# Head memsets, a scaling moved off GpSimd, and the last block's chain in the list scheduler: one change to a fused attention and MLP kernel

## The chip, the cores and the metric

The kernel runs on one core of a Trainium2 chip. A core has TensorE (PE, matrix products into PSUM), VectorE (DVE), ScalarE (ACT), GpSimd (POOL), SyncE (SP, which here only issues transfers) and 16 DMA engines. The metric is the device time of one execution in microseconds. A profile of one execution comes with it; its times count from the start of the profiled span.

## The reference

The input x has 2048 rows of 512 numbers in bf16. It is normalised, goes through an attention of 32 heads of width 16 and, beside it, through a mixer that normalises once more and multiplies along the rows. All three are added.

```python
xn = _layernorm(x)
# attention: H = 32, Dh = 16, no mask
qkv = (xn @ wqkv).reshape(B, S, 3, H, Dh).transpose(2, 0, 3, 1, 4)
p = softmax(einsum("bhqd,bhkd->bhqk", q, k) * Dh ** -0.5)
a = einsum("bhqk,bhkd->bhqd", p, v) -> (B, S, 512) @ wo
# mixer along the rows: F = 1376
u = gelu(einsum("bsd,sf->bdf", _layernorm(xn), w1) + b1)
y = (einsum("bdf,fs->bds", u, w2) + b2).transpose(0, 2, 1)
return x + a + y
```

## The kernel before

**Tiling.** The attention is cut into 32 blocks: 4 query blocks of 512 rows by 8 groups of 4 heads. A block goes over 16 key tiles of 128 rows; each gives two score tiles of 128 keys by 2 heads by 512 queries, so there are 32 x 16 x 2 = 1024 score tiles of 128x1024, numbered n. For each one TensorE writes scores into one of three PSUM slots (L741). ScalarE takes the exponential into a bf16 buffer (L765), or VectorE makes an approximate one: an integer conversion with a bias (L776) and then three copies of it shifted by constants, on VectorE (L785) or GpSimd (L782, an `int64_add` from a library that GpSimd must load first). All four terms are multiplied with V and summed, the last with VM, a scaled copy of V. So a score tile costs one group of P V products (four of 128x256, L808) if ScalarE took it and four groups if VectorE did. V and VM hold 17 columns a head: 16 of values and a one, which makes the softmax sum come out as a 17th row. Where two of the four heads' columns have to be zero, V and VM are cleared.

**Order.** Nothing is scheduled on the chip. A class `Sched` keeps one list of instructions per engine, works out the semaphores from which tile each reads and writes, and keeps a planned time for every engine from written costs. VectorE and GpSimd operations marked `port` are planned not to overlap; beyond the plan, a GpSimd operation waits for the last marked VectorE operation that was emitted ahead of it. Three stretches are written:

1. The head. x tiles are loaded by SP and ScalarE's queue; the first four are normalised (`ln_stats`, `ln_rstd` on GpSimd with a power, `ln_norm` at L549 on VectorE), transposed by TensorE and projected. GpSimd writes ones into V (L659) and zeros into VM (L458, L460); VectorE writes zeros into V (L446, L448).
2. Block 0, in 16 fixed periods, one per key tile: two score tiles, two exponentials on ScalarE, two groups of P V products, and `block0_work`, which normalises, transposes and projects the key tiles two to five ahead. After periods 2, 8, 12 and 15 `vm_scale` (L618) fills VM from V on GpSimd. After period 13 `ln2_stats` (L557 to L561) prepares the second normalisation on GpSimd, whose factors 16 VectorE operations (L565) apply later. After the last period, `late_consts` loads GpSimd's library, clears wo_t on GpSimd (L499), and has SP load wo_c and, into the cleared wo_t, parts of wo; two loads of w1 follow.
3. The list-scheduled loop, for blocks 1 to 31 and the mixer. At each step it collects what each engine could do next, estimates starts, and emits the earliest. Besides scores, exponentials and P V products it handles tasks that are Python generators: Q, K and V projections, the mixer's products, and `task_epilogue`, one per block. The epilogue copies the block's result out of PSUM (L1012), has SP move the softmax sums into dcomp (`den_in`, four transfers) and the values into oC (`o_in`, eight), takes the reciprocal (L1027), writes it to DRAM (`den_mid`), reads it back spread out into denb (`den_out`, four), and after each second block multiplies (two operations at L1048). For block 30, the second-last, it multiplies on its own, half of the rows.

Where the plan leaves TensorE idle and no mixer or projection task is open, it issues products whose result nobody reads (fillers, L1333 and L1339).

Whether VectorE may take a score tile is tested with `n % BN > D_LAST`, with BN = 32 and D_LAST = 31.

After the loop come the standard library on GpSimd and `tail`, which finishes block 31 by itself: VectorE transposes the result (L1075), takes the reciprocal of its sums (L1078), and for each of two halves spreads them out by a transpose (L1082) and multiplies (L1085). TensorE multiplies with wo_t and wo_c into four PSUM banks (L1101, L1090), VectorE (L1113) and ScalarE (L1110) add the rest, and four transfers write the last 512 rows.

The softmax here doesn't subtract the row's maximum and nothing guards it: scores larger than these inputs give would overflow.

## Time and profile before

| | us |
|---|---|
| Median of 3 runs (lowest, highest) | 697.96 (697.03, 698.59) |
| The profiled execution's own time | 698.68 |
| Its span, first to last instruction | 696.9 |
| PE busy in the span | 678.8 (97%) |
| ACT busy | 673.2 (97%) |
| DVE busy | 621.3 (89%) |
| POOL busy | 402.2 (58%) |

A row of the profile's costliest groups gives a line, an engine, an operation, what it writes and reads with the shapes, and a count; then the busy time of all of them in us, the mean of one in ns, the time in which the engine stood idle just before them, and what ended most of that. In a row of the timeline, the first number is the start and the second the duration; what stands in brackets is idle time ahead of it. A row of the chain that ended last gives a start, a duration and what filled it. PE counts as busy when its pipelined products overlap, so its 97% is not a measure of its peak. GpSimd's durations are rough.

### The profile page before, as it was taken

Reading aid. Unit: us, or ns where it says so; the run is one execution under the profiler, and the core shown is the slowest. Engines: PE = TensorE matmul, PEld = TensorE weight load, DVE = VectorE, ACT = ScalarE, POOL = GpSimd, SP = SyncE. Lnnn points to the kernel's source line nnn. Section 1 sums busy time; section 2 is a strip of 40 time slices with the busy share of each in tenths; the row PEclk is TensorE's granted clock in tenths of the full one; section 3 lists DMA queues with packets and bytes.
Section 4 is the critical chain, followed back from the end, with each engine's and each line's share of the span. In section 5 each row is a group of like instructions: output and inputs, shape, how many; then the busy total and the mean of one; then the engine's idle time right before and its main releaser. Section 6 shows DMA issues by size and latency. Waiting matters only on the chain.

```text
span 696.9 us, 29358 instructions
## 1 busy us (share of the span) xinstructions
PE 678.8 (97%) x12916; PEld 312.0 (45%) x12916; DVE 621.3 (89%) x894; ACT 673.2 (97%) x736; POOL 402.2 (58%) x683
## 2 busy tenths in 40 slices
PE   7999999999999999999999999999999999999997
PEld 4433545445544444444444444444444444444443
DVE  7968998998989999989999999898998888888987
ACT  4999999999999999999999999999999999999993
POOL 4544556665356755756666576665766665654642
PEclk9999999999999999999999999999999999999999
DMA  7104200031102200022220212222220222213101
GB/s 211 33 4 82 54 22 20 19 72 28 25 13 52 47 23 19 19 55 46 50 39 22 48 38 54 53 56 53 52 60 20 54 54 57 70 35 81 45 23 44
DMA packets 85728, 32.32 MB, mean 46 GB/s; under 512 B 67424, under 2 KB 85600, under 8 KB 85600
## 3 DMA queue, kind: packets, MB, share of 16 engines
q1 hardware_dynamic: 85168, 30.05, 18.6%
q8 instruction: 101, 1.65, 1.0%
q10 hardware_dynamic: 432, 0.39, 0.2%
q14 instruction: 27, 0.22, 0.1%
HBM read 21.76 MB, written 2.35 MB: 35 GB/s over the span
## 4 chain that ended last, share of the span: by engine, by line
PE 80%; ACT 12%; DVE 4%; DMA 2%; issue 1%; POOL 0%; SPq 0%; DVEq 0%
PE ps L808 32%; PE ps L741 29%; PE ps L839 15%; ACT pT L765 8%; ACT x_sb L765 3%; PE ps L893 2%; DMA denb<-rden_scratch 1%; DVE pT L776 1%; DVE OT L1012 1%; ACT gT_sb L950 1%; DVE hx L549 0%; SPq L431 0%; DMA x_sb<-in_A_x_dram 0%; PE ps L590 0%; DVE oT L1048 0%
## 5 line engine op out<-in xcount | busy, mean ns | idle before, releaser
L765 ACT ACTIVATE pT<-ps 128x1024 bf16<-128x1024 f32 x535 | 523.2, 1132 | 3.3 <-PE ps L741 2.7
L776 DVE TENSOR_SCALAR pT<-ps 128x1024 int16<-128x1024 f32 x221 | 270.1, 1222 | 26.8 <-PE ps L741 20.8
L741 PE MATMUL ps<-QT,KT 32*128 32x512 bf16 x2048 | 284.8, 385 | 5.3 <-ACT pT L765 3.5
L782 POOL INT64_ADD pT<-pT x299 | 181.6, 616 | 129.5 <-DVE pT L785 74.2
L808 PE MATMUL ps<-pT,V 128*32 128x256 bf16 x4716 | 243.8, 276 | 2.9 <-DVE OT L1012 2.5
L765 ACT ACTIVATE x_sb<-ps 128x1024 bf16<-128x1024 f32 x182 | 197.9, 1141 | 0.2 <-PE ps L741 0.2
L741 PEld LDWEIGHTS ps<-QT,KT 32*128 32x128 bf16 x2048 | 78.8, 91 | 183.5 <-ACT pT L765 76.3
L808 PEld LDWEIGHTS ps<-pT,V 128*32 128x32 bf16 x4716 | 107.9, 96 | 85.8 <-issue 66.8
L782 POOL INT64_ADD x_sb<-pT x146 | 89.3, 616 | 57.0 <-DVE pT L785 32.7
L776 DVE TENSOR_SCALAR x_sb<-ps 128x1024 int16<-128x1024 f32 x86 | 105.1, 1222 | 14.7 <-PE ps L741 11.8
L808 PE MATMUL ps<-x_sb,V 128*32 128x256 bf16 x1836 | 116.7, 275 | 1.0 <-DVE OT L1012 0.6
L782 POOL INT64_ADD pT<-x_sb x132 | 79.9, 614 | 48.2 <-DVE pT L785 32.6
L785 DVE TENSOR_SCALAR pT<-pT 128x1024 int16<-128x1024 int16 x154 | 65.1, 426 | 4.5
L808 PE MATMUL ps<-pT,VM 128*32 128x256 bf16 x880 | 61.3, 275 | 0.5 <-DVE pT L785 0.5
L839 PE MATMUL ps<-gT_sb,wblk 128*32 128x512 bf16 (+1 forms) x704 | 61.2, 383 | 0.0
L808 PEld LDWEIGHTS ps<-x_sb,V 128*32 128x32 bf16 x1836 | 46.2, 96 | 31.0 <-issue 23.5
L839 PE MATMUL ps<-hx,wblk 128*32 128x512 bf16 x594 | 52.4, 383 | 0.0
L782 POOL INT64_ADD x_sb<-x_sb x47 | 28.6, 614 | 23.8 <-DVE pT L785 8.0
L847 PE MATMUL ps<-hx,wblk 32*128 32x512 bf16 (+1 forms) x96 | 37.1, 387 | 0.0
L785 DVE TENSOR_SCALAR x_sb<-pT 128x1024 int16<-128x1024 int16 x64 | 27.1, 428 | 1.8
L808 PEld LDWEIGHTS ps<-pT,VM 128*32 128x32 bf16 x880 | 23.3, 96 | 10.6 <-issue 8.8
L785 DVE TENSOR_SCALAR pT<-x_sb 128x1024 int16<-128x1024 int16 x58 | 24.5, 423 | 1.6
(113 smaller groups left out, 460.4 us busy)
## 6 DMA issues: line engine op xcount, KB each, us to landing
wblk<-in_B_w_dram SPq DMA_DIRECT2D x10, 512.0 KB, 4.4
wblk<-in_B_w_dram SPq DMA_DIRECT2D x16, 320.0 KB, 3.6
oC<-OT SPq DMA_DIRECT2D x248, 16.0 KB, 1.8
denb<-rden_scratch SPq DMA_DIRECT2D x124, 32.0 KB, 2.3
xr<-in_A_x_dram SPq DMA_DIRECT2D x16, 128.0 KB, 2.6
dcomp<-OT SPq DMA_DIRECT2D x124, 2.0 KB, 1.7
QT<-Qall SPq DMA_DIRECT2D x120, 16.0 KB, 1.8
out_dram<-osb SPq DMA_DIRECT2D x14, 128.0 KB, 2.0
```

Source lines behind the costliest of these rows:

```text
L741: specs.append(dict(eng="pe", fn=lambda e, r=r, bk=bk: e.matmul(bank(bk), lhsT=KT[32 * r:32 * r + 32, T, 128 * kt:128 * (kt + 1)], rhs=QT[ ...
L765: return [dict(eng="act", fn=lambda e: e.activation(buf(pbuf[n]), ps[:, s_ * 1024:(s_ + 1) * 1024], ACTF.Exp, scale=LN2_128), reads=[("ban ...
L776: return dict(eng="dve", fn=lambda e: e.tensor_scalar(buf_i(w), ps[:, s_ * 1024:(s_ + 1) * 1024], IBIAS, 0.0, ALU.add, ALU.max), reads=[(" ...
L782: return dict(eng=eng, fn=lambda e: e.int64_add(buf_i(o).bitcast(I64), buf_i(w).bitcast(I64), SHIFTS[k] * 0x0001000100010001), reads=[("pT ...
L785: return dict(eng=eng, fn=lambda e: e.tensor_scalar(buf_i(o), buf_i(w), float(SHIFTS[k]), 1.0, ALU.add, ALU.mult), reads=[("pT", w)], writ ...
L808: specs.append(dict(eng="pe", fn=lambda e, c=c, h=h, i=i, off=off: e.matmul(bank(PV_BANK)[32 * c:32 * c + 32, 256 * par:256 * par + 256], ...
L839: specs.append(dict(eng="pe", fn=lambda e, c=c, w=w: e.matmul(bank(EX_BANK)[32 * c:32 * c + w, :], lhsT=lhs_of(32 * c, 32 * c + w), rhs=rh ...
L847: return [dict(eng="pe", fn=lambda e: e.matmul(bank(EX_BANK)[0:dst_rows, :], lhsT=lhs_of(0, dst_rows)[rs], rhs=rhs[rs], start=begin, stop= ...
L893: return [dict(eng="pe", fn=lambda e, ct=ct, c=c: e.matmul(bank(EX_BANK)[32 * c:32 * c + 32, 128 * i:128 * (i + 1)], lhsT=xnT[:, ct, 128 * ...
L950: yield "act", [dict(eng="act", fn=lambda e, ap=ap: e.activation(ap, ap, ACTF.Gelu_apprx_tanh), reads=[("gT", f) for f in fts], writes=[(" ...
L1012: yield "pvev", [dict(eng="dve", fn=lambda e: e.tensor_copy(OT32[:, eb, :], bank(PV_BANK)), reads=[("bank", PV_BANK)], writes=[("OT32", eb)])]
```

## The change

The diff has these parts.

- The ones of V (L659) and the zeros of wo_t (L499) are written by VectorE at the very start. The zeros of V are written by GpSimd, in a function that also does VM's: V's before the first statistics, VM's at the old place.
- The first normalisation is emitted before the statistics of tile 3, the other three after them.
- `vm_scale` of periods 12 and 15 goes to VectorE. `ln2_stats` and `late_consts` are both called after period 12.
- A score tile is kept from VectorE if `n >= 1022`, in place of the old test.
- The epilogue's `o_in` transfers become a generator of their own. For block 30 it runs beside the rest of the epilogue; for the others it runs inside it as before. A new gate makes the multiplication wait, in the plan, for the emission of these transfers.
- The chain of block 31 on VectorE moves from `tail` into `task_last`, which the loop schedules like other tasks.
- The planner keeps a list of the last eight busy intervals of the shared port for each engine instead of one time until which it is taken.
- PER_LIST is 16, the number of periods, so the tests against it leave the periods as they are, and `next_n` starts at 32 as before.

```diff
-D_LAST = 31
+D_END = 1022
@@ Sched
-    def port_time(self, eng, t):
-        return max(t, self.port_free["pool" if eng == "dve" else "dve"])
+    def port_time(self, eng, t, dur):
+        for a, z in self.port_iv["pool" if eng == "dve" else "dve"]:
+            if t < z and t + dur > a:
+                t = z
+        return t
...
-            self.port_free[eng] = op.t0 + cost[0]
+            self.port_iv[eng] = self.port_iv[eng][-7:] + [(op.t0, op.t0 + cost[0])]
@@ head
-        for T in range(1, 4):
-            sc.add("dve", lambda e, T=T: e.memset(v17_kh[:, :, 8 * T, 0:16], 0.0),
-                   writes=[("V", t, T) for t in range(NT)], cost=(0.15, 0.2))
-        sc.add("dve", lambda e: e.memset(V17[:, NKT * H * 17:], 0.0), writes=[("V", NKT, 0)], cost=(0.06, 0.1))
+        sc.add("dve", lambda e: e.memset(v17_main[:, :, 16:17], 1.0), writes=[("Vone",)], cost=(0.5, 0.55))
+        sc.add("dve", lambda e: e.memset(wo_t[:], 0.0), writes=[("wo_t", z) for z in range(4)], cost=(0.92, 0.97))
...
-        def late_memsets():
+        def zero_memsets(nm, whole, kh):
             for T in range(1, 4):
-                sc.add("pool", lambda e, T=T: e.memset(vm_kh[:, :, 8 * T, 0:16], 0.0),
-                       writes=[("VM", t, T) for t in range(NT)], cost=(0.3, 0.4))
-            sc.add("pool", lambda e: e.memset(VM[:, NKT * H * 17:], 0.0), writes=[("VM", NKT, 0)], cost=(0.1, 0.2))
+                sc.add("pool", lambda e, T=T: e.memset(kh[:, :, 8 * T, 0:16], 0.0),
+                       writes=[(nm, t, T) for t in range(NT)], cost=(0.3, 0.4))
+            sc.add("pool", lambda e: e.memset(whole[:, NKT * H * 17:], 0.0), writes=[(nm, NKT, 0)], cost=(0.1, 0.2))
...
             load_lib(INT64_LIB)
-            sc.add("pool", lambda e: e.memset(wo_t[:], 0.0), writes=[("wo_t", z) for z in range(4)], cost=(1.75, 1.8))
...
+        zero_memsets("V", V17, v17_kh)
         ln_sums(1)
...
         ln_rstd(1, 2)
+        ln_norm(0)
         ln_stats(3)
-        sc.add("pool", lambda e: e.memset(v17_main[:, :, 16:17], 1.0), writes=[("Vone",)], cost=(2.28, 2.33))
-        for t in range(NPRE):
+        for t in range(1, NPRE):
             ln_norm(t)
-        late_memsets()
+        zero_memsets("VM", VM, vm_kh)
@@ block 0
-                vm_scale(list(range(4 * j, 4 * j + 4)), 0)
-            if period == 13:
+                vm_scale(list(range(4 * j, 4 * j + 4)), 0, "pool" if period < LN2_AT else "dve")
+            if period == LN2_AT:
                 ln2_stats()
-        late_consts()
+                late_consts()
@@ task_epilogue
-            yield "gate", lambda: p < 2 or PAIRS[p - 2] in oT_done
-            for c in range(4):
-                h, i = divmod(c, 2)
-                for a in range(2):
-                    ro = 64 * e_ + 32 * a + 16 * i
-                    yield "sp", [dict(dst=oC32[ro:ro + 16, tb_, 256 * h:256 * h + 256],
-                                      src=OT32[32 * c:32 * c + 16, eb, 256 * a:256 * a + 256],
-                                      reads=[("OT32", eb)], writes=[("oC32", tb_, e_, c, a)], name="o_in")]
-            yield "call", lambda: ot_free.add(b)
+            g_in = dict(gen=task_o_in(b), cur=None)
+            if b == NBLK - 2:
+                yield "call", lambda: (step_gen(g_in), frees.append(g_in))
+            else:
+                yield from task_o_in(b)
...
+            yield "gate", lambda: b in ot_free and (half or b - 1 in ot_free)
@@ the loop
-                    if n % BN > D_LAST or (qi == 0 and len(ready_q) == 1 and False):
+                    if n >= D_END:
                         continue
...
                     if pv_block == NBLK - 1:
                         pv_block += 1
+                        g = dict(gen=task_last(), cur=None)
+                        step_gen(g)
+                        frees.append(g)
```

`task_o_in` holds the gate and the eight transfers as they stood; `task_last` holds the six VectorE operations of `tail` (transpose, reciprocal, and twice the spreading transpose and the product) as they stood, each as a task step. LN2_AT is 12.

## The prediction

> **What bounds the kernel now.** I read the page's engine rows first, then its costliest groups, then the chain that ended last at both ends of the run, then the timeline where the chain shows a hole. All clock times below are microseconds from the span's start in the profile of before.
>
> ```profile
> PE 678.8 (97%) x12916; PEld 312.0 (45%) x12916; DVE 621.3 (89%) x894; ACT 673.2 (97%) x736; POOL 402.2 (58%) x683
> ...
> L765 ACT ACTIVATE pT<-ps 128x1024 bf16<-128x1024 f32 x535 | 523.2, 1132 | 3.3 <-PE ps L741 2.7
> L776 DVE TENSOR_SCALAR pT<-ps 128x1024 int16<-128x1024 f32 x221 | 270.1, 1222 | 26.8 <-PE ps L741 20.8
> ...
> L765 ACT ACTIVATE x_sb<-ps 128x1024 bf16<-128x1024 f32 x182 | 197.9, 1141 | 0.2 <-PE ps L741 0.2
> ```
>
> There are 1024 exponentials of 128x1024. ScalarE (L765) takes 535 + 182 = 717 of them, VectorE (L776) 221 + 86 = 307. ScalarE waits only 3.5 us before all of its 717, so from its first exponential to its last it is the pacing engine. The timeline gives these ends: the first starts at 15.27, the last (of four merged, 681.11 + 3.92) ends at 685.03. That is 669.76 us, in which the view by windows counts 660.91 us of L765. Taking off one table load of 1.28 merged into it leaves 659.6 / 717 = 0.92 us per exponential. So the span falls into three pieces: 15.27 us of head, 669.76 us paced by ScalarE, and 696.9 - 685.03 = 11.87 us of tail. I price the change in each.
>
> The chain in the head:
>
> ```profile
> 7.15 0.63 POOL mv L529
> 7.79 0.03 issue
> 7.81 3.10 DVE hx L549
> 10.92 0.05 issue
> 10.96 0.40 PE ps L577 x4
> ```
>
> The last of the four first normalisations (L549) takes 3.10 us where the median of its 16 is 0.382. The timeline of GpSimd shows what stands beside it:
>
> ```profile
> 7.73 2.27 POOL L659 MEMSET V<- 128x512 bf16 x1
> 9.59 1.12 POOL L458 MEMSET VM<- 128x256 bf16 x3
> 10.64 0.12 POOL L460 MEMSET VM<- 128x16 bf16 x1
> ```
>
> VectorE's normalisation is released only after GpSimd's last memset, at 10.76. Everything after it (transposes, projections, first scores, first exponential) hangs on it in order.
>
> In the early middle, the timelines of VectorE and GpSimd show this:
>
> ```profile
> 38.46 0.42 DVE L573 CAST V<-ps 128x256 bf16<-128x256 f32 x1
> ...
> 46.23 1.22 DVE L776 TENSOR_SCALAR x_sb<-ps 128x1024 int16<-128x1024 f32 x1 [3.16 <-PE ps L741]
> ...
> 51.04 4.28 DVE L565 TENSOR_SCALAR hx<-hx,mv 128x512 bf16<-128x512 bf16 x16
> 55.95 1.23 DVE L776 TENSOR_SCALAR pT<-ps 128x1024 int16<-128x1024 f32 x1 [0.62 <-PE ps L741]
> ...
> 42.51 0.65 POOL L618 TENSOR_SCALAR VM<-V 128x544 bf16<-128x544 bf16 x1 [0.73 <-DVE V L573]
> 48.71 1.79 POOL L499 MEMSET wo_t<- 128x2048 bf16 x1 [5.55 <-issue]
> ```
>
> VectorE takes one exponential at 46.23 and none again until 55.95. GpSimd loads its library in the 5.55 us ahead of 48.71, then clears wo_t for 1.79; VectorE's 16 renormalisations fill 51.04 to 55.32.
>
> The chain at the end:
>
> ```profile
> 684.85 3.27 DMA denb<-rden_scratch
> ...
> 688.19 0.43 DVE wkv_raw L1048
> ...
> 688.65 0.42 DVE wkv_raw L1048
> 689.06 0.64 DVE denb L1075
> ```
>
> The last exponential on ScalarE was over at 685.03, but the last block's chain on VectorE (L1075 to L1085) starts at 688.99. It stands in line behind L1048, which waits for the second-last block's reciprocals to land at 688.12. The last P V product is done at 687.96, held back by the shifts of a VectorE exponential begun at 684.56.
>
> **The change, part by part.**
>
> *Head memsets.* VectorE loses three V memsets of 0.165 and one small one, and gains ones in V (512 elements) and zeros in wo_t (1024 words). Rows L440 (256 words, 0.272) and L446 (128 words, 0.165) give 0.84 ns a word and 0.06 fixed, so the two take about 0.49 and 0.92: VectorE is done at about 2.6, and its next work starts with the first x tile at 3.48. Hidden, with 0.9 us of cover; beyond it every us goes into the path. GpSimd gets V's zeros, three at 0.32 and one at 0.12, after qmask at 2.69: done at about 3.8, its next work comes at 4.48. Hidden, 0.7 us of cover.
>
> *The blocked normalisation.* One normalisation (0.38) now stands before tile 3's statistics, which makes the last GpSimd power end at about 7.95 instead of 7.78. Then VM's four memsets follow, and they collide with the fourth normalisation as V's did. [...] the normalisation sat through the whole back-to-back train to 10.76, not to the end of the first memset at 10.0. By the row it waits 7.95 + 0.95 (three of 0.26 apart, then 0.12) and ends near 9.06: gain 10.91 - 9.06 = 1.85. I take the row. [...] if the train is as long as the rows' sum of 1.24, 1.55. What follows needs x tiles 4 and 5 and the first weights: issued by 3.7 and landed 4 to 4.5 us later, so not late.
>
> *V scaling and library.* Two of the four scalings (0.65 each on GpSimd) become VectorE instructions of 0.30 (the 12 such rows have 301 ns). The second-layernorm chain on GpSimd is moved one period up, but it now waits for the first of them, behind the V copy that ends at 38.88: it starts near 39.2 instead of 37.83, takes the same 3.96, and the library load of 5.55 runs from 43.2 to 48.7, where it ran before. So the library is not earlier; only the wo_t memset of 1.79 goes, and with it one VectorE shift that was held for 1.68 instead of 0.43. What moves is the 16 renormalisations: free at 43.2, done at 47.5, over VectorE's former idle 3.16. Late next is the copy of block 0's result (47.37 before, about 48.8 now) and so block 1's first P V product; TensorE ran six filler products there, which cover it, and without them it would cost 1.4. From 47.5 to 56.0 VectorE then has 8.5 us, less 1.4 for two copies, at 1.9 us per exponential with its shift: 3.7 instead of 1, so about three more. On SP the four wo_t loads waited 29.2 us for that memset (before 50.5), with two w1 loads of 512 KB and the Q rows behind them. Now the 12 loads of wo (8 + 4) and the two of w1 go out around 17 to 26, when the transfers' share is about 0.14; nothing waits for them then.
>
> *Last two exponentials.* D_END keeps scores 1022 and 1023 off VectorE; one was there before. The old bound of 31 never excluded anything, since n % 32 is at most 31. Three more less one is two, and the two instruction streams say the same: ScalarE 717 to 715, VectorE 307 to 309. Gain in the paced piece: 2 x 0.92 = 1.84. The streams also have six more P V groups of 0.11 and six fewer fillers of 0.22 on TensorE, which is even or better.
>
> *Tail.* Last exponential ends, its P V products 0.4 later (VectorE's last shift is done by about then), the transpose 0.15 after that, since L1048 no longer stands ahead. From the transpose to the end took 696.9 - 688.99 = 7.91. The two products of L1048 now stand between the two halves of the last block's chain; one output product on TensorE needs the second of them, which is one VectorE step of 0.42 later than its place before. Sum 0.4 + 0.15 + 7.91 + 0.42 = 8.88 instead of 11.87: gain 3.0. The moved product must find its reciprocals: SP issues den_mid after five o_in instead of eight (0.72 each), with three o_in behind it, so the denb loads start near 682.7 rather than 683.56 and land near 687.25. The product is due near 688.8. Cover 1.5; beyond it, one for one. Between 1.5 (the last shift decides again) and 3.6.
>
> *Port as intervals* alters only the planner's own estimates; what it does is in the counts above. Its unknown is how well the new order fits the chip: ScalarE's idle in the paced piece is about 2.2 us now, so from a gain of 1.5 to a loss of 3; I take nothing.
>
> **Sum.** 1.85 + 1.84 + 3.0 = 6.7. Against the profiled execution: span 696.9 to 690.2, time 698.68 to 692.0. That execution is 0.7 above the median, so against the median 697.96 - 6.7 = 691.3. About 0.2% (1.4 us) is what the measurement tells from no change.
>
> **Rivals.**
>
> 1. *The middle gives nothing*: TensorE is as busy as ScalarE (97%), and the two exponentials become ScalarE waiting for scores. For: the chain is 80% TensorE. Against: ScalarE waits 3.5 us in all. Time 697.96 - 4.85 = 693.1, to 694.6 if it idles 1.5 more.
> 2. *The head is not shortened*: VectorE's memsets run past 3.48, or the VM train holds the normalisation longer. Against: cover of 0.9. Time 697.96 - 4.84 = 693.1.
> 3. *Slower*: the replanned order meets the chip badly, and ScalarE waits for scores in every block, at the block changes where TensorE stands behind the result copy. At 0.25 us a block, 31 blocks make 7.8: 699.1. It decides from 6.7 us of added wait, three times all its present idle. The even windows (49.6 to 50.0 of each 50 us) speak against it.
> 4. *The change doesn't do what it says*: two scalings leave GpSimd, and the library still comes no earlier. The renormalisations move earlier all the same. If VectorE's second exponential stays late, ScalarE waits where the plan had counted on it: one exponential lost is 0.92, 692.2, inside the first case's own range.
>
> **How the numbers follow.** All three parts: 0.63, around 691.3, own range 689.8 to 692.8. Rival 1 0.20, rival 2 0.08, slower 0.05; the remaining 0.04 is a mixture that ends within 0.2%. Faster 0.63 + 0.20 + 0.08 = 0.91, same 0.04, slower 0.05. The range for 8 in 10 goes from 689.0 ([...]full tail gain) to 694.8 (rival 1 with its added wait).
>
> **What would show it.** The fourth normalisation near 1.2 us instead of 3.10 and the first exponential near 13.4; 715 exponentials on ScalarE with an idle of about 2; VectorE's second exponential before 52; the transpose of the last block within 0.7 us of ScalarE's last exponential, and 8.9 us from there to the end. Wrong if ScalarE's waits for TensorE exceed 6, if the first x statistics start after 3.6, or if the moved product waits for its reciprocals.

## The result, and the profile after

The changed kernel takes 691.96 us (median of four runs, 691.73 to 692.20). The kernel before, run on the same chip, takes 698.28 (four runs, 697.03 to 699.07). The ratio is 0.9911, with a 95% interval of 0.9894 to 0.9928. That is faster by 6.3 us, against 6.7 forecast, and 691.96 against 691.3. The profiled execution of after took 692.2, its span is 690.4.

The total came out; of its three terms only the tail did. I cut both spans at the same two points, ScalarE's first and last exponential:

| | before | after | gain | forecast |
|---|---|---|---|---|
| Head, to the first exponential | 15.27 | 12.52 | 2.75 | 1.85 |
| Paced piece, first to last exponential | 669.76 | 669.35 | 0.41 | 1.84 |
| Tail, from there to the end | 11.87 | 8.53 | 3.34 | 3.0 |
| Span | 696.9 | 690.4 | 6.5 | 6.7 |

In after.py most lines lie a little further down: the exponential of ScalarE is L768 (L765 before), that of VectorE L779 (L776), the scores L744 (L741), the normalisation of the head L551 (L549), the last block's transpose L1086 (L1075), the epilogue's products L1061 (L1048).

The engine rows and the groups of exponentials of after, in the columns of those shown before:

```profile
PE 674.3 (98%) x12934; PEld 309.7 (45%) x12934; DVE 618.7 (90%) x895; ACT 672.3 (97%) x734; POOL 401.7 (58%) x690
...
L768 ACT ACTIVATE pT<-ps 128x1024 bf16<-128x1024 f32 x535 | 521.1, 1126 | 2.7 <-PE ps L744 2.1
...
L768 ACT ACTIVATE x_sb<-ps 128x1024 bf16<-128x1024 f32 x180 | 194.0, 1130 | 0.6 <-PE ps L744 0.5
```

ScalarE takes 535 + 180 = 715 exponentials, as forecast, and waits 3.3 us before them where it waited 3.5. But part of both stands ahead of the first exponential, in the head; these are its rows before and after:

```profile
15.27 1.02 ACT L765 ACTIVATE pT<-ps 128x1024 bf16<-128x1024 f32 x1 [1.35 <-PE ps L741]
```

```profile
12.52 3.77 ACT L768 ACTIVATE pT<-ps 128x1024 bf16<-128x1024 f32 x4 [0.48 <-PE ps L744]
```

So inside the paced piece the waits grew, from 3.5 - 1.35 = 2.15 to 3.3 - 0.48 = 2.82.

The head on VectorE and on GpSimd, from two timelines of after:

```profile
2.84 0.48 DVE L450 MEMSET V<- 128x512 bf16 x1 [1.70 <-issue]
3.47 0.91 DVE L451 MEMSET wo_t<- 128x1024 uint32 x1
4.30 0.63 DVE L521 BATCH_NORM_STATS2 stats<-x_sb 128x6 f32<-128x512 bf16 x1
...
8.52 0.87 DVE L551 TENSOR_SCALAR hx<-x_sb,mv 128x512 bf16<-128x512 bf16 x1 [0.17 <-POOL mv L531]
```

```profile
7.90 0.58 POOL L531 TENSOR_TENSOR mv<-mv,mhalf 128x1 f32<-128x1 f32 x1
8.43 0.81 POOL L461 MEMSET VM<- 128x256 bf16 x3
9.18 0.25 POOL L463 MEMSET VM<- 128x16 bf16 x1
```

The fourth normalisation takes 0.87 instead of 3.10, as meant. But the first statistics start at 4.30 where 3.48 was forecast: ahead of the ones memset stands a hole of 1.70 that I had not priced. So the normalisation ends at 9.39, not 9.06.

The renormalisations and VectorE's next exponentials, from the timeline of after:

```profile
40.39 4.29 DVE L567 TENSOR_SCALAR hx<-hx,mv 128x512 bf16<-128x512 bf16 x16 [0.38 <-POOL mv L563]
44.60 1.22 DVE L779 TENSOR_SCALAR x_sb<-ps 128x1024 int16<-128x1024 f32 x1
...
47.79 1.23 DVE L779 TENSOR_SCALAR pT<-ps 128x1024 int16<-128x1024 f32 x1
```

The 16 operations moved from 51.04 to 40.39 and VectorE's second exponential from 55.95 to 47.79, as the prediction had it ("before 52"). Of the 10.65 by which the renormalisations come earlier, 2.75 is the shorter head; the other 7.9 is the step from 51.04 to 43.2 that the prediction had on the clock of before.

The tail on ScalarE and on VectorE:

```profile
674.28 7.59 ACT L768 ACTIVATE pT<-ps 128x1024 bf16<-128x1024 f32 x8
```

```profile
682.28 0.72 DVE L1086 STREAM_TRANSPOSE denb<-ps 128x512 f32<-128x512 f32 x1 [0.86 <-PE ps L811]
...
684.49 0.38 DVE L1061 TENSOR_TENSOR wkv_raw<-oC,denb 64x256 bf16<-64x256 f32 x1
```

ScalarE's last exponential is over at 681.87. The transpose of block 31 starts 0.41 later (forecast 0.55), with the products of block 30 no longer ahead of it; these two run at 684.49 and 685.13 and wait for nothing. From the transpose to the end it is 8.12 (forecast 8.33).

### The profile page after: what moved, and what is told of

It is laid out like the page before. It is cut to its first block, busy times and chain, and to the rows that moved or that the text cites. A ratio compares the mean times of both kernels' runs of the same rounds, so it can differ in the third digit from the quotient of the medians.

```text
span 690.4 us, 29398 instructions
## 1 busy us (share of the span) xinstructions
PE 674.3 (98%) x12934; PEld 309.7 (45%) x12934; DVE 618.7 (90%) x895; ACT 672.3 (97%) x734; POOL 401.7 (58%) x690
## 4 chain that ended last, share of the span: by engine, by line
PE 78%; ACT 13%; DVE 5%; issue 1%; POOL 1%; SPq 0%; DMA 0%; DVEq 0%
PE ps L811 32%; PE ps L744 28%; PE ps L842 14%; ACT pT L768 10%; ACT x_sb L768 2%; PE ps L896 1%; DVE pT L779 1%; DVE OT L1028 1%; ACT gT_sb L953 1%; DVE hx L567 1%; DVE oT L1061 0%; SPq L436 0%; DMA denb<-rden_scratch 0%; POOL mv L563 0%; PE ps L648 0%
## 5 line engine op out<-in xcount | busy, mean ns | idle before, releaser
L768 ACT ACTIVATE pT<-ps 128x1024 bf16<-128x1024 f32 x535 | 521.1, 1126 | 2.7 <-PE ps L744 2.1
L779 DVE TENSOR_SCALAR pT<-ps 128x1024 int16<-128x1024 f32 x222 | 271.2, 1222 | 28.0 <-PE ps L744 21.2
L744 PE MATMUL ps<-QT,KT 32*128 32x512 bf16 x2048 | 283.1, 384 | 6.0 <-ACT pT L768 3.0
L785 POOL INT64_ADD pT<-pT x319 | 193.0, 613 | 117.1 <-DVE pT L788 77.5
L811 PE MATMUL ps<-pT,V 128*32 128x256 bf16 x4728 | 249.4, 276 | 3.5 <-DVE OT L1028 3.1
L768 ACT ACTIVATE x_sb<-ps 128x1024 bf16<-128x1024 f32 x180 | 194.0, 1130 | 0.6 <-PE ps L744 0.5
L744 PEld LDWEIGHTS ps<-QT,KT 32*128 32x128 bf16 x2048 | 78.2, 91 | 183.7 <-ACT pT L768 69.8
L811 PEld LDWEIGHTS ps<-pT,V 128*32 128x32 bf16 x4728 | 110.3, 96 | 87.3 <-issue 68.8
L785 POOL INT64_ADD x_sb<-pT x142 | 86.6, 613 | 70.0 <-DVE pT L788 32.2
L779 DVE TENSOR_SCALAR x_sb<-ps 128x1024 int16<-128x1024 f32 x87 | 106.3, 1221 | 8.8 <-PE ps L744 6.7
L785 POOL INT64_ADD pT<-x_sb x115 | 70.1, 618 | 45.7 <-DVE pT L788 27.9
L788 DVE TENSOR_SCALAR pT<-pT 128x1024 int16<-128x1024 int16 x148 | 62.9, 427 | 4.3
L785 POOL INT64_ADD x_sb<-x_sb x55 | 33.4, 612 | 21.7 <-DVE pT L788 11.9
L788 DVE TENSOR_SCALAR pT<-x_sb 128x1024 int16<-128x1024 int16 x65 | 27.3, 427 | 1.8
L788 DVE TENSOR_SCALAR x_sb<-pT 128x1024 int16<-128x1024 int16 x57 | 23.9, 420 | 1.5
```

The lines of the kernel that those rows point to most:

```text
L744: specs.append(dict(eng="pe", fn=lambda e, r=r, bk=bk: e.matmul(bank(bk), lhsT=KT[32 * r:32 * r + 32, T, 128 * kt:128 * (kt + 1)], rhs=QT[ ...
L768: return [dict(eng="act", fn=lambda e: e.activation(buf(pbuf[n]), ps[:, s_ * 1024:(s_ + 1) * 1024], ACTF.Exp, scale=LN2_128), reads=[("ban ...
L779: return dict(eng="dve", fn=lambda e: e.tensor_scalar(buf_i(w), ps[:, s_ * 1024:(s_ + 1) * 1024], IBIAS, 0.0, ALU.add, ALU.max), reads=[(" ...
L785: return dict(eng=eng, fn=lambda e: e.int64_add(buf_i(o).bitcast(I64), buf_i(w).bitcast(I64), SHIFTS[k] * 0x0001000100010001), reads=[("pT ...
L788: return dict(eng=eng, fn=lambda e: e.tensor_scalar(buf_i(o), buf_i(w), float(SHIFTS[k]), 1.0, ALU.add, ALU.mult), reads=[("pT", w)], writ ...
L811: specs.append(dict(eng="pe", fn=lambda e, c=c, h=h, i=i, off=off: e.matmul(bank(PV_BANK)[32 * c:32 * c + 32, 256 * par:256 * par + 256], ...
```

## The experiments

Twelve kernels were run, each from the changed kernel with one thing undone or altered, or from the kernel before with one thing added. None leaves out a part of the result. "Against after" sets a median beside 691.96. The ratios are to the kernel before on the same chip. These runs were spread over four chips, and the runs of before with a mean clock of 0.999 or more have medians of 697.0, 697.1, 697.1 and 697.9 on them, so a difference "against after" of less than about 1 us is not read as an effect.

### The head: what gave 2.75, and what held it up

From the normalisation's end to the first exponential before needs 15.27 - 10.91 = 4.36, after 12.52 - 9.39 = 3.13, for the same products. Here is the group of TensorE's products that opens this window before, and then its window with its granted clock (us, busy time and count, clock, DMA share, GB/s), before:

```profile
L577 PE MATMUL ps<-ident,hx 128*128 128x128 bf16 x4 | 0.4, 222 | 2.5 <-DVE hx L549 2.5
```

```profile
10.96:15.30 4.34, 4.34 (x44) 0.65 0.87 223
```

And after:

```profile
9.40:12.50 3.10, 3.02 (x44) 1.00 1.08 358
```

The same 44 products take 4.34 before and 3.10 after: in before's profile TensorE had a clock of 0.65 there, after standing idle for 2.51 us behind the blocked normalisation, and a product of 128x128 (the K and V projections) took 288 ns instead of 219. The shorter block left only 0.31 idle ahead of the same products. Is the clock really the cause of 1.2 us, and does the idle stretch bring it? I filled the idle stretch in the kernel before, and nothing else:

**clock_fill**, from the kernel before:

```diff
-N_MID = (1, 1, 1, 2)
+N_MID = (1, 1, 8, 2)
```

> The kernel before with seven more warm-up products on TensorE in the gap ahead of the fourth tile's transposes (N_MID's third entry 8 instead of 1). Theory C (the gap of 2.5 us lowers TensorE's clock, and that costs 1.2 us on its own): the clock is 1.00 through 11 to 15, the projection products have a mean near 219 ns instead of 311, the first exponential starts at about 14.1, time about 1.2 below the kernel before. Theory D (the products there wait for data or transfers, not for a clock): the first exponential stays at 15.3 and the time within 0.4 of the kernel before.

The timeline of clock_fill on TensorE, and on ScalarE its first exponential:

```profile
8.08 1.89 PE L646 MATMUL ps<-pT 128*128 128x512 bf16 x8
10.98 0.40 PE L577 MATMUL ps<-ident,hx 128*128 128x128 bf16 x4 [1.01 <-DVE hx L549]
```

```profile
14.06 1.94 ACT L765 ACTIVATE pT<-ps 128x1024 bf16<-128x1024 f32 x2 [0.49 <-PE ps L741]
```

The normalisation is as late as before (the transposes behind it start at 10.98), the idle stretch is 1.01, the clock is 1.00, and the first exponential starts at 14.06 instead of 15.27, as forecast. The median of 12 runs is 697.20 (ratio 0.9991, 0.9982 to 1.0), far less than the 1.2 that this profile shows. The reason lies in the kernel before: of 48 of its runs whose clock is listed, 24 have a mean granted clock of 0.999 or 1.0 and a median of 697.15, the other 24 one of 0.997 or 0.998 and a median of 698.60. A clock of 0.65 over 4.34 us takes 0.002 off the mean of the whole span (4.34 x 0.35 / 697), which is what separates the groups. So, as far as the mean clock tells, the dip comes in half of its executions and costs 1.45; the profiled one had it. The profile of before_port (below) has the same head with an idle stretch of 2.5 and no dip: its clock stays at 1.00 and its first exponential starts at 13.78. Filling the idle stretch removes the dip: none of 12 runs of clock_fill has a mean clock under 0.999 or is above 697.63. Against before without the dip, the change brings about 697.15 - 691.96 = 5.2, across chips.

Next, the head's part of the change was undone, with wo_t's zeros left on VectorE:

**head_old**, from after:

```diff
-        sc.add("dve", lambda e: e.memset(v17_main[:, :, 16:17], 1.0), writes=[("Vone",)], cost=(0.5, 0.55))
+        for T in range(1, 4):
+            sc.add("dve", lambda e, T=T: e.memset(v17_kh[:, :, 8 * T, 0:16], 0.0),
+                   writes=[("V", t, T) for t in range(NT)], cost=(0.15, 0.2))
+        sc.add("dve", lambda e: e.memset(V17[:, NKT * H * 17:], 0.0), writes=[("V", NKT, 0)], cost=(0.06, 0.1))
...
-        zero_memsets("V", V17, v17_kh)
-        ln_norm(0)
         ln_stats(3)
-        for t in range(1, NPRE):
+        sc.add("pool", lambda e: e.memset(v17_main[:, :, 16:17], 1.0), writes=[("Vone",)], cost=(2.28, 2.33))
+        for t in range(NPRE):
             ln_norm(t)
```

> The changed kernel with the ones of V back on GpSimd between tile 3's statistics and the normalisations, V's zeros back on VectorE, the old order of the normalisations; everything else as changed, and the order of instructions after the head is the same. Theory A (the memset train on GpSimd holds the fourth normalisation, and TensorE, idle meanwhile, comes back at a lower clock): the fourth normalisation takes about 3.1 us, the granted clock behind it is near 0.65, the first exponential starts about 2.7 later (15.3), and the time is about 694.7. Theory B (the head is hidden behind something that paces the run, and the gain came from the middle and the tail): the time stays within 0.5 of 692.0.

Measured: 693.48 (692.81 to 694.09), ratio to before 0.9940 (0.9923 to 0.9958), 1.5 against after. GpSimd and VectorE in its timelines:

```profile
7.60 2.26 POOL L664 MEMSET V<- 128x512 bf16 x1
9.46 1.25 POOL L464 MEMSET VM<- 128x256 bf16 x3
10.66 0.11 POOL L466 MEMSET VM<- 128x16 bf16 x1
```

```profile
6.34 4.12 DVE L554 TENSOR_SCALAR hx<-x_sb,mv 128x512 bf16<-128x512 bf16 x4
```

The block is back: four normalisations take 4.12 and end near 10.46. The time came back by 1.5 and not 2.7: the idle stretch of TensorE is 2.20 here, the profile has a clock of 1.00 behind it, and only one of the four runs, 694.09, has a mean clock under 0.999. The first exponential starts at 13.60, 1.08 after that of after. The block itself is worth about 1.1 to 1.5, the clock another 1.2 to 1.45 in about half of the executions of before. This profile also says something on who waits for whom: here the normalisation ended within the train of VM memsets, before its last.

Then the hole of 1.70 ahead of the ones. Is it a wait before the first bigger operation, whichever that is, or a cost of the ones? I swapped the two memsets:

**swap**, from after:

```diff
-        sc.add("dve", lambda e: e.memset(v17_main[:, :, 16:17], 1.0), writes=[("Vone",)], cost=(0.5, 0.55))
         sc.add("dve", lambda e: e.memset(wo_t[:], 0.0), writes=[("wo_t", z) for z in range(4)], cost=(0.92, 0.97))
+        sc.add("dve", lambda e: e.memset(v17_main[:, :, 16:17], 1.0), writes=[("Vone",)], cost=(0.5, 0.55))
```

> The changed kernel with VectorE's two head memsets in the other order (zeros of wo_t first, then ones of V). Theory E (a stall of VectorE's instruction stream behind its second instruction, whatever comes third): the third instruction, now the zeros of wo_t, starts near 2.84, and the first statistics again start near 4.3; time about 692. Theory F (the ones of V waited for GpSimd's operations, which end at 2.68): the zeros of wo_t run from 1.15 to 2.05, the ones from about 2.84 to 3.3, the first statistics start near 3.5 and the time is about 0.8 lower.

The timeline of swap on VectorE:

```profile
1.30 0.91 DVE L450 MEMSET wo_t<- 128x1024 uint32 x1 [0.16 <-issue]
3.92 0.48 DVE L451 MEMSET V<- 128x512 bf16 x1 [1.71 <-issue]
4.04 0.63 DVE L521 BATCH_NORM_STATS2 stats<-x_sb 128x6 f32<-128x512 bf16 x1
```

Measured 691.56 in one run. Neither theory holds: wo_t starts at once, and the 1.71 went with the ones to their new place. It belongs to this memset. It writes 512 single bf16 elements 34 bytes apart; 1.70 + 0.48 = 2.18 is 4.3 ns an element, and the same memset on GpSimd took 2.26 in the profile of head_old above. (In swap the statistics start at 4.04, within the memset's own row, so there it held VectorE up for 1.83.) The type is not what costs: in after, a memset of 512 bf16 elements that lie side by side, though on one partition only, has the same 0.48 of its own and no such hole:

```profile
36.49 0.48 DVE L512 MEMSET gT_sb<- 1x512 bf16 x1 [0.16 <-issue]
```

To see whether the cost goes by the element, I took head_new (next) and cut the ones in two:

**ones_split**, from head_new:

```diff
-        sc.add("dve", lambda e: e.memset(v17_main[:, :, 16:17], 1.0), writes=[("Vone",)], cost=(0.5, 0.55))
+        for u in range(2):
+            sc.add("dve", lambda e, u=u: e.memset(v17_main[:, 256 * u:256 * u + 256, 16:17], 1.0), writes=[("Vone",)], cost=(0.25, 0.28))
```

> head_new with VectorE's ones in V written by two memsets of 256 elements instead of one of 512. In all three runs with that memset on VectorE the engine stood 1.70 idle ahead of it. Theory K (the strided write costs by the element, and the idle is part of it): each of the two has about 0.85 idle and 0.25 of its own, together 2.2. Theory L (a fixed cost of every such instruction): 1.7 ahead of each, together 3.9, first statistics near 5.0. Theory M (a cost of its first use): 1.7 ahead of the first alone. The time says nothing here, as head_new's first x tile lands at 3.3 in K and M.

The timeline of ones_split on VectorE:

```profile
1.96 0.27 DVE L451 MEMSET V<- 128x256 bf16 x1 [0.82 <-issue]
3.17 0.27 DVE L451 MEMSET V<- 128x256 bf16 x1 [0.94 <-DVE V L451]
```

Half the elements, half the hole (0.82 and 0.94) and half the shown time (0.27 each): the cost goes by the element, at 0.82 + 0.27 = 1.09 and 0.94 + 0.27 = 1.21 for 256, 4.3 and 4.7 ns. Measured 691.73 in one run, no better than head_new. Why most of the cost stands as idle time ahead of the instruction is not shown.

With that, wo_t's zeros need not stand on VectorE at all. In head_new GpSimd writes them, with VM's zeros, only after the fourth normalisation and the statistics of tile 4:

**head_new**, from after:

```diff
-        sc.add("dve", lambda e: e.memset(wo_t[:], 0.0), writes=[("wo_t", z) for z in range(4)], cost=(0.92, 0.97))
...
-        zero_memsets("VM", VM, vm_kh)
...
         ln_stats(NPRE)
+        zero_memsets("VM", VM, vm_kh)
+        sc.add("pool", lambda e: e.memset(wo_t[:], 0.0), writes=[("wo_t", z) for z in range(4)], cost=(1.75, 1.8))
```

> The changed kernel with the zeros of wo_t taken from VectorE's start and written by GpSimd behind the zeros of VM, and both of these moved behind the statistics of tile 4. Theory A: the first statistics start near 3.5 instead of 4.3, the fourth normalisation takes 0.38 instead of 0.87, so the first exponential starts 1.3 earlier (about 11.2) and the time is about 690.7. Theory B': the first exponential is held by the weights or x tiles instead, and starts at 12.2 or later; time 691.6 or more.

The timelines of head_new on VectorE and on ScalarE:

```profile
3.35 0.69 DVE L520 BATCH_NORM_STATS2 stats<-x_sb 128x6 f32<-128x512 bf16 x1
...
7.74 0.41 DVE L550 TENSOR_SCALAR hx<-x_sb,mv 128x512 bf16<-128x512 bf16 x1 [0.17 <-POOL mv L530]
```

```profile
11.29 1.02 ACT L768 ACTIVATE pT<-ps 128x1024 bf16<-128x1024 f32 x1 [0.49 <-PE ps L744]
```

Measured 690.33 (690.17 to 690.73), ratio to before 0.9897 (0.9877 to 0.9916), 1.6 better than after. The statistics start at 3.35, the fourth normalisation takes 0.41, the first exponential starts at 11.29, 1.23 before that of after. So the two things that kept the head from more, the late statistics and the rest of the block, are worth 1.23 in the head, and the change could have had them.

### The middle: what gave the two exponentials

The prediction put them down to the renormalisations, moved forward by the scalings that leave GpSimd and by wo_t's memset that is gone. I undid the scalings and the place of the second normalisation, and left wo_t where it is:

**mid_old**, from after:

```diff
-                vm_scale(list(range(4 * j, 4 * j + 4)), 0, "pool" if period < LN2_AT else "dve")
-            if period == LN2_AT:
+                vm_scale(list(range(4 * j, 4 * j + 4)), 0)
+            if period == 13:
                 ln2_stats()
-                late_consts()
+        late_consts()
```

> The changed kernel with the two V scalings back on GpSimd, the second layernorm's statistics back behind period 13 and the library load back behind the last period; wo_t's zeros stay on VectorE at the start, and the head, the port intervals and the tail stay as changed. Its instruction lists again give ScalarE 715 exponentials and VectorE 309. Theory A (ScalarE paces, so only its count matters): within 0.4 of 692.0. Theory G (as the prediction told it, VectorE freed by this edit is what takes the two exponentials over): slower by 1.8, 693.8, with ScalarE waiting longer between 45 and 56.

The groups of exponentials of mid_old, and its renormalisations:

```profile
L768 ACT ACTIVATE pT<-ps 128x1024 bf16<-128x1024 f32 x516 | 504.4, 1126 | 2.5 <-PE ps L744 1.9
...
L768 ACT ACTIVATE x_sb<-ps 128x1024 bf16<-128x1024 f32 x199 | 212.4, 1129 | 0.5 <-PE ps L744 0.4
```

```profile
40.33 4.29 DVE L567 TENSOR_SCALAR hx<-hx,mv 128x512 bf16<-128x512 bf16 x16
```

Measured 691.37 (691.17 to 691.50), ratio 0.9915 (0.9900 to 0.9930). There are still 516 + 199 = 715 exponentials on ScalarE, and the time is no longer (0.6 shorter; the medians of before above differ by up to 0.9 between chips). The renormalisations are as early as in after (40.33, there 40.39). So neither the scalings nor the place of the second normalisation is what moved them: that half of the prediction's theory falls.

The other candidate is the port, "intervals" or a single time in the planner, which the prediction had at nothing:

**port_old**, from after (and the two places that keep the intervals):

```diff
-        for a, z in self.port_iv["pool" if eng == "dve" else "dve"]:
-            if t < z and t + dur > a:
-                t = z
-        return t
+        return max(t, self.port_free["pool" if eng == "dve" else "dve"])
```

> The changed kernel with the planner's single time until which the shared port is taken, in place of the list of intervals; everything else as changed. Its instruction lists give ScalarE 719 exponentials and VectorE 305. Theory A (ScalarE paces at 0.92 each): four more on ScalarE, slower by 3.7, about 695.6. Theory H (TensorE paces as much: 12 fewer groups of P V products at 0.11 are 1.3 less for it): within 0.7 of 692.0.

The groups of exponentials of port_old:

```profile
L765 ACT ACTIVATE pT<-ps 128x1024 bf16<-128x1024 f32 x508 | 500.1, 1130 | 3.5 <-PE ps L741 2.0
...
L765 ACT ACTIVATE x_sb<-ps 128x1024 bf16<-128x1024 f32 x211 | 225.1, 1136 | 0.2 <-PE ps L741 0.2
```

Measured 695.61 (12 runs, 694.82 to 697.19), ratio 0.9966 (0.9956 to 0.9976), 3.65 against after; forecast 3.7. ScalarE has 719 exponentials, four more, and at 0.92 these are the 3.7. The renormalisations come at 45.92, and VectorE's first exponential only at 52.09. But the size is not clean: this kernel also has a window with a low clock (busy time and count of PE, PEld, DVE, ACT and POOL, then the clock), where after has none. The first fence is port_old, the second after:

```profile
45.00:60.00 15.00, 12.52 (x154) 3.79 (x152) 9.82 (x23) 13.40 (x15) 2.70 (x5) 0.77 0.09 20
```

```profile
45.00:60.00 15.00, 14.27 (x273) 6.01 (x271) 13.92 (x20) 14.46 (x17) 8.46 (x14) 1.00 0.08 17
```

A plan without this stall was wanted, and undoing both parts makes one:

**mid_port_old**, both edits, of which these lines are the core:

```diff
-        for a, z in self.port_iv["pool" if eng == "dve" else "dve"]:
+        return max(t, self.port_free["pool" if eng == "dve" else "dve"])
...
-            if period == LN2_AT:
+            if period == 13:
                 ln2_stats()
-                late_consts()
+        late_consts()
```

> The changed kernel with both parts that could have shaped the middle undone together: V scalings and library load at their old places, and the planner's single port time. wo_t's zeros stay on VectorE, head and tail as changed. ScalarE has 718 exponentials, VectorE 306. Theory A (ScalarE's count alone, 0.92 each): 2.8 slower than the changed kernel, 694.7, its waits for TensorE as few as there (2.6 in all). Theory O (the single port time costs by stalls as well, as in port_old): waits above 3.5 or a mean clock under 0.998, and a time of 695.3 or more. Theory P (the middle of before was as good): within 0.7 of 692.0.

The groups of exponentials of mid_port_old, and its renormalisations:

```profile
L765 ACT ACTIVATE pT<-ps 128x1024 bf16<-128x1024 f32 x549 | 535.1, 1142 | 2.0 <-PE ps L741 1.5
...
L765 ACT ACTIVATE x_sb<-ps 128x1024 bf16<-128x1024 f32 x169 | 184.4, 1143 | 0.3 <-PE ps L741 0.2
```

```profile
47.06 4.28 DVE L564 TENSOR_SCALAR hx<-hx,mv 128x512 bf16<-128x512 bf16 x16
```

Measured 695.27 (695.25 to 695.34), ratio 0.9956 (0.9939 to 0.9973), 3.3 against after; its profile's span is 2.8 longer, 693.2 against 690.4. The clock is 1.00, ScalarE hardly waits (2.3 in all), and it has 549 + 169 = 718 exponentials. Its paced piece is 671.02 against 669.35, 1.7 longer, and its tail 9.65 against 8.53, 1.1 longer. So without the low clock too, the intervals are worth about 3 us within this change: somewhat more than half in the paced piece (three exponentials at 0.92 would be 2.8), the rest in how the last block falls out. Waits alone do not explain it: the forecast that had them at 3.5 or more is refuted, though its time was near.

Is it then the intervals that give the two exponentials? I put them alone into the kernel before:

**before_port**, from the kernel before:

```diff
-        return max(t, self.port_free["pool" if eng == "dve" else "dve"])
+        for a, z in self.port_iv["pool" if eng == "dve" else "dve"]:
+            if t < z and t + dur > a:
+                t = z
+        return t
```

> The kernel before with the list of port intervals and nothing else. Its instruction lists give ScalarE 718 exponentials and VectorE 306, where the kernel before has 717 and 307. Theory A (ScalarE's count sets the pace, and the intervals pay only together with the wo_t memset's removal from GpSimd): 0.9 slower than the kernel before. Theory N (the intervals are what shortens the middle, whatever else is changed): 1.8 or more faster than the kernel before.

The timelines of before_port on VectorE and on ScalarE, and TensorE's clock in three windows (stretch and length, clock, DMA share, GB/s):

```profile
47.53 2.19 DVE L788 TENSOR_SCALAR x_sb<-x_sb 128x1024 int16<-128x1024 int16 x2
```

```profile
50.48 1.02 ACT L768 ACTIVATE pT<-ps 128x1024 bf16<-128x1024 f32 x1 [1.94 <-PE ps L744]
```

```profile
55.27:75.27 20.00, 0.94 0.24 44
75.27:95.27 20.00, 1.00 0.22 47
95.27:115.27 20.00, 0.83 0.11 24
```

Measured 704.37 (700.66 to 704.89), ratio 1.0083 (1.0054 to 1.0112): slower than before by 6.5, with 718 exponentials. No theory of the expectation had a loss of this size. In its profile wo_t's memset on GpSimd, from 47.32 to 49.11, falls on VectorE's shifts, two of which take 2.19 where two in after take 0.75; the P V products then wait 1.10 for them, and ScalarE 1.94 for its scores. TensorE's clock falls twice: to 0.94 and 0.72 from 50 to 60, and, after 40 us at 1.00, to 0.72 and 0.60 from 100 to 110. The second time has another cause: VectorE stood for 1.81 until 100.19 in a product that waits for its reciprocals, its next exponential came late, and TensorE was idle for 1.58 ahead of 102.27. ScalarE waits 8.3 us for scores in the whole run where before it waited 2.7, 2.5 of it from 50 to 58 and 3.9 from 104 to 112. The order in time is shown, and the change has no memset near 47 (it is at the very start). That the collision brought the first low clock is an inference, and no run undoes either stall alone.

Put beside each other, the six kernels separate the parts. The renormalisations are timed from ScalarE's first exponential, so that the head drops out; the last column counts VectorE's exponentials among the first 1000 score tiles in their order in the trace.

| | port | zeros of wo_t | scalings of periods 12, 15 | renormalisations start | VectorE's of 1000 |
|---|---|---|---|---|---|
| before | single time | GpSimd, middle | GpSimd | 35.8 | 299 |
| mid_port_old | single time | VectorE, start | GpSimd | 34.5 | 299 |
| port_old | single time | VectorE, start | VectorE | 33.4 | 298 |
| before_port | intervals | GpSimd, middle | GpSimd | 27.8 | 299 |
| mid_old | intervals | VectorE, start | GpSimd | 27.8 | 302 |
| after | intervals | VectorE, start | VectorE | 27.9 | 302 |

The intervals move the renormalisations, by 5.5 to 8 us, whatever else is changed. The reason can be read in the code: with a single time the planner puts a VectorE operation marked `port` behind the planned end of the last GpSimd operation emitted ahead of it, here one that follows the library load; with intervals it may stand before it. The three more exponentials come only where, besides, wo_t's zeros are gone from GpSimd's middle; with the one of the last two that VectorE no longer takes they make the forecast two. The scalings make no difference to either. The rows differ in head and tail too, and the changed kernel with wo_t's zeros alone put back was not run. In time the intervals are worth about +3 in the changed kernel, half of its gain, and -6.5 in the one before.

Last of the middle, the two edits that were better than the change, together:

**head_new_mid_old**, both edits, of which these lines are the core:

```diff
-        sc.add("dve", lambda e: e.memset(wo_t[:], 0.0), writes=[("wo_t", z) for z in range(4)], cost=(0.92, 0.97))
...
+        sc.add("pool", lambda e: e.memset(wo_t[:], 0.0), writes=[("wo_t", z) for z in range(4)], cost=(1.75, 1.8))
...
-            if period == LN2_AT:
+            if period == 13:
                 ln2_stats()
-                late_consts()
+        late_consts()
```

> The changed kernel with both edits of head_new (zeros of wo_t and VM on GpSimd behind tile 4's statistics) and of mid_old (the V scalings and library load at their old places). ScalarE has 715 exponentials. If the two effects add, head_new's 1.6 and mid_old's 0.6: about 689.7, first exponential near 11.3. If mid_old's 0.6 was scatter: about 690.3.

Measured 690.15 (689.78 to 690.66), ratio 0.9889 (0.9873 to 0.9906), 0.2 under head_new, whose runs it overlaps. The 0.6 of mid_old does not add to the 1.6 of head_new, so I take nothing from it. Head_new and this one beat both kernels, before and after.

### The tail: the last two exponentials, and the chain

**dend_old**, from after:

```diff
-D_END = 1022
+D_END = 4096
```

> The changed kernel with VectorE allowed to take the last two score tiles (D_END 4096). The order is the same up to the last tile; ScalarE has 714 exponentials, VectorE 310. Theory A (the tail waits for the last shifts): ScalarE's last exponential ends 0.9 earlier, VectorE's last shift and the last P V products come about 2.6 later behind it, the last block's transpose starts 1.7 later, time about 693.6. Theory I (the last block's chain waits for the reciprocals or TensorE anyway): within 0.4 of 692.0.

The timeline of dend_old on VectorE:

```profile
682.87 0.42 DVE L788 TENSOR_SCALAR x_sb<-pT 128x1024 int16<-128x1024 int16 x1
683.69 0.72 DVE L1086 STREAM_TRANSPOSE denb<-ps 128x512 f32<-128x512 f32 x1 [0.40 <-PE ps L811]
```

Measured 693.69 (693.62 to 693.94), ratio 0.9949 (0.9934 to 0.9964), 1.7 against after, as forecast. VectorE takes one score tile more (310), its last shift runs until 683.29, and the transpose starts at 683.69, not 682.28. ScalarE is done at 680.71, 1.2 earlier, and the tail is 2.7 longer; the balance is 1.5 in the spans and 1.7 in the medians. Here an exponential that relieved ScalarE by 0.92 cost more than it gave, as its shifts were the last thing that the P V products waited for.

**last_old**, from after:

```diff
-            if b == NBLK - 2:
-                yield "call", lambda: (step_gen(g_in), frees.append(g_in))
-            else:
-                yield from task_o_in(b)
+            yield from task_o_in(b)
...
         def tail():
+            for kind_, specs_ in task_last():
+                for z_ in specs_:
+                    add(z_)
...
-                        g = dict(gen=task_last(), cur=None)
-                        step_gen(g)
-                        frees.append(g)
```

> The changed kernel with the last block's chain emitted behind everything else again and block 30's value transfers again ahead of its reciprocal; D_END stays 1022. Theory A (the second-last block's product stands ahead and waits for its reciprocals to land): that product starts near 683.6 instead of 684.5, the last block's transpose near 684.5 instead of 682.3, time 1.8 slower, about 693.8. Theory J (the reciprocals land in time and the product merely takes its 0.86): 0.4 slower, about 692.4.

The timelines of last_old on VectorE and on TensorE:

```profile
684.39 0.87 DVE L1058 TENSOR_TENSOR wkv_raw<-oC,denb 64x256 bf16<-64x256 f32 x2 [3.22 <-DMA denb<-rden_scratch]
685.18 0.70 DVE L1083 STREAM_TRANSPOSE denb<-ps 128x512 f32<-128x512 f32 x1
```

```profile
687.16 1.04 PE L1118 MATMUL ps<-wo_t,oT 128*128 128x512 bf16 x4 [2.64 <-DVE oT L1092]
```

Measured 695.13 (8 runs, 693.46 to 696.43), ratio 0.9968 (0.9955 to 0.9981), 3.2 against after, where 1.8 was forecast. The products of block 30 are back ahead of the transpose and wait 3.22 for their reciprocals. The runs whose mean clock is 0.999 or 1.0 took 693.46 to 694.71, those with 0.997 or 0.998 took 695.55 to 696.43. The profile is of the second kind; its window of all engines (stretch and length, then busy time and count of PE, PEld, DVE, ACT and POOL, TensorE's clock, DMA share, GB/s):

```profile
687.00:692.00 5.00, 4.04 (x12) 1.30 (x12) 2.87 (x6) 0.60 (x1) 0.00 (x0) 0.66 0.16 52
```

TensorE stands idle for 2.64 while the late chain runs, and in the next 5 us, with the output products, its clock is 0.66. The four runs without the low clock have a median of 694.3, so without it the edit costs about 2.3. The edit undoes two things at once, the place of the chain and that of `o_in`; with `o_in` ahead, SP issues the reads of the reciprocals from 679.94 instead of 678.72, and how the 2.3 splits is not shown.

## Why the prediction came out

**The total was right because errors cancelled.** The head gave 0.9 more than forecast, the tail 0.3 more, the paced piece 1.4 less. That they met at 6.5 of 6.7 is luck: 1.2 of the head is a dip of the clock which the prediction did not have, and which only about half of the executions of before show. Without it the three pieces give 5.3, and the medians 5.2.

**Head, right in mechanism; two terms mis-sized and one missing.** "The two take about 0.49 and 0.92: VectorE is done at about 2.6 ... Hidden" is the step that failed. It took a rate of 0.84 ns a word from rows whose words lie side by side, or in runs of eight, and applied it to 512 single elements 34 bytes apart. These took 2.18, not 0.49, and the prediction's own row had 2.27 for the same memset on GpSimd; with wo_t behind them the statistics came 0.82 late. This was the mechanism of the rival in which the head is not shortened, and it did come, at a smaller price: the last GpSimd power ended at 8.48 instead of 7.95. The prediction had named the sign itself ("if the first x statistics start after 3.6"); they started at 4.30. The runs put this memset at 4.3 to 4.7 ns an element; none tried another stride.

On the blocked normalisation I took the row of before, by which it waits for the whole memset train. In after the train runs from 8.43 to 9.43, and by the row the normalisation would end after that. It ended at 9.39, having taken 0.87, 0.46 longer than the same operation in head_new (0.41), where no memset stands beside it: held up, but sooner than the row. In head_old it ended within the train too, near 10.46, before its last memset (10.66). So the row is not confirmed. GpSimd's durations are too rough to say which memset it passed.

The term that the sum did not have is the clock. The profile of before showed it, in a window that the prediction did not use: 0.65 from 10.96 to 15.30, after 2.51 us in which TensorE stood idle. About half of the executions (24 of 48) show such a dip in their mean, and in this profile it put 1.2 on the head.

**Paced piece: the count right, the time wrong, and one link of the cause.** ScalarE has 715 exponentials as forecast, but "2 x 0.92 = 1.84" brought 0.41. About 0.7 of the missing 1.4 is ScalarE's added waits inside the piece, 2.82 after 2.15. They vary between executions of one order of instructions: head_new, swap and ones_split have that of after in this piece, and their profiles have pieces of 668.70, 668.97 and 669.95 beside 669.35 (before 669.76, clock_fill with its order 670.22). A difference of 0.4 between two single profiles says little. The rest I could not locate.

"What moves is the 16 renormalisations" is confirmed, and their place too. What was wrong is what moves them. The prediction tied it to wo_t's memset going and to the scalings leaving GpSimd; mid_old keeps the early renormalisations with the scalings where they were. The step that failed is "*Port as intervals* ... I take nothing": the table shows that the intervals move them, and that the three exponentials need them. Undone in the changed kernel they cost about 3 to 3.65, and put into the kernel before they cost 6.5. The range given for them, from a gain of 1.5 to a loss of 3, was too narrow on both sides. As the prediction says, their effect was inside the counts that it read from the two instruction streams, and that saved the number.

**Tail, right.** Both halves have a run that undoes them: dend_old makes the tail 2.7 longer for the two exponentials kept off VectorE, and last_old costs 2.3 to 3.2 for the chain. Their sum, 5.0 or more, is over the gain of 3.34, so they overlap. The moved product found its reciprocals, as forecast: SP issued the four reads from 678.72 to 680.70, 3.15 ahead of the end of ScalarE's last exponential (2.3 in the forecast, 1.5 before). They landed 2.0 to 3.3 us after their issue, so by about 683.6 (an estimate, 680.28 + 3.3), and the product started at 684.49 without a wait: a cover of about 0.9 where the prediction had 1.5.

**The rivals.** "The middle gives nothing" is near what the two profiles show for that piece, with 0.7 of the added waits that it named. "Slower" did not come for the change, but its mechanism is real: before_port is a replanned order that meets the chip badly, with 5.6 us more of waits for scores than before and 704.37, beyond the 699.1 of that rival.

## What to carry to other kernels

Price a strided memset by its elements at their own stride (here 2.18 us for 512), and look at the idle time ahead of it (1.70) as well as at its own row (0.48). Ask for the granted clock in the windows around every idle stretch of TensorE: a wait can cost a second time, in the products that come after it (the same 44 took 4.34 us at 0.65 and 3.10 at 1.00). And where a planner orders the work, a part of a change has no fixed value: count what the new plan does, undo the parts one at a time and in pairs on the chip, and look where the moved operations stand in each run before a cause is given to a count.

## What the runs showed of the hardware

**The memset of single elements 34 bytes apart cost 4.3 to 4.7 ns an element on VectorE** (2.18 us for 512 in after, 1.09 and 1.21 for 256 in ones_split), and 2.26 us for 512 on GpSimd in head_old. On VectorE the profile of after shows 0.48 of it as the operation and 1.70 as idle time ahead of it. For 512 elements side by side, on one partition, it shows 0.48 and 0.16.

**TensorE's clock fell after idle stretches of 1.58 to 2.64 us, in some executions and not in others.** After 2.51 us it was 0.65 for the next 4.3 us in the profile of before; by their mean clock 24 of 48 runs have such a dip, and it is worth 1.45 in the time. After 2.5 us, in the same head of before_port, it stayed at 1.00, and after 2.20 in the profile of head_old too. With the stretch filled to 1.01 us none of 12 runs was above 697.63. In the tail of last_old 2.64 us were followed by 0.66 over 5 us, by the mean clock in four of eight runs. In before_port 1.58 us at 102 were followed by 0.60 from 105 to 110. In port_old TensorE was busy for 3.04 of the 5 us from 45 to 50, with no single wait above 0.53, and had 0.52 from 50 to 57; all 12 of its runs have a mean clock of 0.998 or less. So the length of one idle stretch alone does not decide it here.
